# Nystrom attention and a multiplicative FFN: loads of q, k and v cut in pieces between other work, and the first batch's turns moved

## The chip, the cores and the metric

The kernel runs on one core of one Trainium2 chip. The core has five engines that run side by side and wait for one another by semaphores: TensorE (PE in the profile), VectorE (DVE), ScalarE (ACT), GpSimd (POOL) and SyncE (SP). The metric is the device time of one execution in microseconds (us).

## The reference

```python
B, H, S, D = 8, 8, 576, 64;  m = 32;  scale = 1 / 8
q_lm = q.reshape(B, H, m, S // m, D).mean(axis=3)     # 32 landmarks of 18 rows each
k_lm = k.reshape(B, H, m, S // m, D).mean(axis=3)
A, Bm, C = sm(q, k_lm), sm(q_lm, k_lm), sm(q_lm, k)   # softmax of the scaled products
Z = Bm.T / (norm1(Bm) * norminf(Bm) + 1e-6)
for _ in range(6): Z = 2 * Z - Z @ Bm @ Z
attn = A @ Z @ C @ v                                  # per batch and head
x = attn with the heads side by side                  # (4608, 512)
out = (((x @ w1) * (x @ w2)) @ w3) @ w_out            # w1, w2: 512x1024, w3: 1024x1024, w_out: 1024x512
```

All inputs and the output are float32 in memory.

## The kernel before

The work is written out by hand in one order; each engine takes its instructions in the order in which the program issues them, and a tile framework adds the waits. Work is staged by batch, eight batches of 8 heads x 576 rows.

- **Loads.** `load_qk` (L71) brings k and then q of a batch from GpSimd's DMA queue, changing them to float16 on the way, 96 partitions x 8 heads x 384 values. `load_v` (L77) brings v in float32 from SP's queue. Each has two buffers.
- **Turns.** q and k are needed with the head's dimension on the partitions. For batch 0 TensorE turns them (`turn_on_pe`, L100, copied out by L104); for the others SP issues DMA transposes (`transposes`, L89, called by `turn_all`).
- **Landmark sums.** `landmarks` (L166 to L175) adds up the rows of each landmark in six operations into `parts`, once for k and once for q: on GpSimd, or, for q of batch 0, on VectorE in two halves.
- **Attention.** `attention` is a generator of 18 steps; between its steps the caller puts other work on TensorE. Its first step (L183) multiplies `parts`, so it needs the sums of both q and k. Steps 3 and 4 hold the scores of C (L224) and GpSimd's `presum` of them (L235 to L240, then L259 and L262), steps 6 and 7 the product with v (L305), steps 8 to 13 the six iterations (L369), and the last four (L412 to L418) fold the result into w1 and w2 to give `g`.
- **Up.** `up(st, j, w)` (L426) multiplies `g` by the first factor for unit j of 8. The product for w1 is copied out by ScalarE (L430), and VectorE multiplies it by the product for w2 into `ab` (L432). The products use three PSUM buffers named `big`.
- **Down.** `down` (L446) multiplies `ab` by w3 @ w_out, scaled out by ScalarE (L452) and written by SP (L459). An even batch has 8 half products, an odd one 10.
- **Fold.** `fold` makes w3 @ w_out (`w34`) in the first stage, once: 64 steps (`product`, L490), with turns of w3 on TensorE (`turn`, L477, copied out by L482 and L483).

The first stage issues the loads of the weights, of q and k of batch 0, and then mixes the fold's steps with the turns, sums and attention of batch 0. Two one-column copies on GpSimd (L565, L571) read q or k of batch 0 and write into the buffer of a load that follows, so that this load waits for them: a gate. After it, the loop over batches runs `up(b)` with attention of batch b+1 between the units, then the sums for batch b+2, then `down(b)` with the rest of attention b+1, and at its end the first step of attention b+2 (`steps(nxt)`).

Of the kernel before, what the change touches and what calls it, by code (L numbers as in the profile page):

```python
# [7 lines left out]
FP32 = mybir.dt.float32  # L8
FP16 = mybir.dt.float16
# [4 lines left out]
B = 8  # L14
H = 8
# [6 lines left out]
DF = 1024  # L22
# [3 lines left out]
NP = 96  # L26
# [5 lines left out]
def kernel(  # L32
# [11 lines left out]
    nc = tc.nc  # L44
    consts = ctx.enter_context(tc.tile_pool(name="consts", bufs=1))
    wpool = ctx.enter_context(tc.tile_pool(name="wpool", bufs=1))
    pin = ctx.enter_context(tc.tile_pool(name="pin", bufs=2))
# [5 lines left out]
    def big():  # L53
        return psp.tile([128, 2, 512], FP32, name="big", bufs=3)
# [13 lines left out]
    def load_qk(st, b):  # L68
        qkn = pin.tile([128, 2, H, 384], FP16, name="qkn")
        for t, src in ((1, k), (0, q)):  # L70
            nc.gpsimd.dma_start(out=qkn[0:NP, t, :, :],  # L71
                                in_=src[b].rearrange("h (p r) d -> p h (r d)", p=NP))
        st["qkn"] = qkn

    def load_v(st, b):
        vt = st["vt"] if "vt" in st else pin.tile([128, H, 384], FP32, name="vt")
        nc.sync.dma_start(out=vt[0:NP], in_=v[b].rearrange("h (p r) d -> p h (r d)", p=NP))  # L77
        st["vt"] = vt

    def load_weight(t, w):  # L80
        for qd in range(2):
            nc.gpsimd.dma_start(out=wup[64 * qd:64 * qd + 64, :, t, :],
                                in_=w[256 * qd:256 * qd + 256, :].rearrange("(h d) j -> d h j", d=D))
# [10 lines left out]
    def turn_on_pe(st, t, h0, copy):  # L94
        if "qkT" not in st:
            st["qkT"] = pat.tile([128, 2, H, 3, NP], FP16, name="qkT")
        ps = psp.tile([128, 2, 1024], FP16, name="big", bufs=3)
        for i in range(2):
            for n in range(6):
                nc.tensor.transpose(  # L100
                    out=ps[:, i, NP * n:NP * n + NP],
                    in_=st["qkn"][0:NP, t, h0 + 2 * i + n // 3, 128 * (n % 3):128 * (n % 3) + 128],
                    identity=ident16[0:NP, 0:NP])
        copy(out=st["qkT"][:, t, h0:h0 + 4, :, :].rearrange("p (i h) c s -> p i (h c s)", i=2),  # L104
             in_=ps[:, :, 0:6 * NP])
# [49 lines left out]
        return mask4, par, ones, eye2, iit, onesq, selc, lomask  # L155


    def landmarks(st, t, eng=nc.gpsimd):
        if "parts" not in st:
            st["parts"] = pz.tile([128, 2, 2, H, 32], FP16, name="parts")  # L160
        for h0 in ((0,) if eng is nc.gpsimd else (0, 4)):
            own, n = ("", H) if eng is nc.gpsimd else ("v", 4)
            hs = slice(h0, h0 + n)
            x = st["qkT"][:, t, hs, :, :]
            tr = pat.tile([128, n, NP], FP32, name="tr" + own, bufs=1)
            eng.tensor_tensor(out=tr, in0=x[:, :, 0, :], in1=x[:, :, 1, :], op=ALU.add)  # L166
            eng.tensor_tensor(out=tr, in0=tr, in1=x[:, :, 2, :], op=ALU.add)  # L167
            t3 = tr.rearrange("p h (l g) -> p h l g", g=3)
            o = pat.tile([128, n, 32], FP32, name="o3" + own, bufs=1)
            hi, lo = st["parts"][:, 0, t, hs, :], st["parts"][:, 1, t, hs, :]  # L170
            eng.tensor_tensor(out=o, in0=t3[:, :, :, 0], in1=t3[:, :, :, 1], op=ALU.add)
            eng.tensor_tensor(out=o, in0=o, in1=t3[:, :, :, 2], op=ALU.add)  # L172

            eng.tensor_copy(out=hi, in_=o)
            eng.tensor_tensor(out=lo, in0=o, in1=hi, op=ALU.subtract)  # L175
# [334 lines left out]
    sts = [dict() for _ in range(B)]  # L510

    def turn_all(b):
        for t in (1, 0):
            for h0 in (0, 4):
                transposes(sts[b], t, range(h0, h0 + 4))

    def steps(g, n=1):
        for _ in range(n):
            next(g, None)
# [3 lines left out]
    with tc.tile_pool(name="pf", bufs=2) as pf:  # L523
        wof, w3f = {}, {}
        wsp = pf.tile([128, 2, 8, DM], FP16, name="wsp", bufs=1)

        def load_w3(j, cc=None):
            if j not in w3f:
                w3f[j] = pf.tile([128, DF], FP32, name="w3f", bufs=3)
            sl = slice(0, DF) if cc is None else slice(512 * cc, 512 * cc + 512)  # L530
            nc.sync.dma_start(out=w3f[j][:, sl], in_=moe_w3[128 * j:128 * (j + 1), sl])

        def load_wout(i, eng):
            wof[i] = pf.tile([128, 2, DM], FP32, name="wof", bufs=3)
            eng.dma_start(out=wof[i],
                          in_=moe_w_out[256 * i:256 * i + 256, :].rearrange("(c p) f -> p c f", p=128))

        load_w3(0, 0)
        load_wout(0, nc.scalar)
        load_w3(1, 0)  # L540
        load_wout(1, nc.scalar)
        load_w3(0, 1)
        load_wout(2, nc.scalar)
        load_w3(1, 1)

        warm = pf.tile([128, 512], FP16, name="warm", bufs=1)
        nc.vector.memset(warm, 0.0)
        psw = big()
        for _ in range(10):
            nc.tensor.matmul(psw[:, 0, :], warm[:, 0:128], warm, start=True, stop=True)  # L550

        nc.gpsimd.tensor_copy(out=gate, in_=wof[1][:, 0, 0:1])
        load_qk(sts[0], 0)
        load_weight(0, moe_w1)
        load_weight(1, moe_w2)
        mask4, par, ones, eye2, iit, onesq, selc, lomask = constants()
        fd = fold(pf, wof, w3f, wsp)
        steps(fd, 1)
        load_wout(3, nc.sync)
        load_w3(2)  # L560
        steps(fd, 6)
        load_w3(3)
        steps(fd, 9)
        w3f[4] = pf.tile([128, DF], FP32, name="w3f", bufs=3)
        nc.gpsimd.tensor_copy(out=w3f[4][0:NP, 0:1], in_=sts[0]["qkn"][0:NP, 1, 0, 0:1])  # L565
        load_w3(4)
        turn_on_pe(sts[0], 1, 0, nc.scalar.copy)
        turn_on_pe(sts[0], 1, 4, nc.vector.tensor_copy)
        landmarks(sts[0], 1)
        sts[0]["vt"] = pin.tile([128, H, 384], FP32, name="vt")  # L570
        nc.gpsimd.tensor_copy(out=sts[0]["vt"][0:NP, 0, 0:1], in_=sts[0]["qkn"][0:NP, 0, 0, 0:1])  # L571
        load_v(sts[0], 0)
        load_qk(sts[1], 1)
        steps(fd, 8)
        turn_on_pe(sts[0], 0, 0, nc.scalar.copy)
        turn_on_pe(sts[0], 0, 4, nc.vector.tensor_copy)
        landmarks(sts[0], 0, nc.vector)
        steps(fd, 3)
        load_w3(5)
        steps(fd, 4)  # L580
        at = attention(sts[0])
        for n, m in enumerate((2, 2, 2, 2, 2, 2, 2, 1, 1, 1, 1, 1, 1, 1, 2, 2, 2, 2, 2, 1)):
            steps(at)
            if n == 3:
                load_w3(6)
            elif n == 7:
                load_w3(7)
                load_v(sts[1], 1)
                turn_all(1)
                landmarks(sts[1], 1)  # L590
                load_qk(sts[2], 2)
                landmarks(sts[1], 0)
            steps(fd, m)
        steps(at, 30)
        steps(fd, 64)
    pab = ctx.enter_context(tc.tile_pool(name="pab", bufs=3))
    at = attention(sts[1], acc)


    for b in range(B):  # L600
        st = sts[b]
        ab = st["ab"] = pab.tile([128, 8, S], FP16, name="ab")
        if b + 2 < B:
            turn_all(b + 2)
            load_v(sts[b + 2], b + 2)
        if b % 2 == 0:
            chunks = [[(b, ab, 128 * t, 128)] for t in range(4)]
        else:
            chunks = [[(b - 1, sts[b - 1]["ab"], 512, 64), (b, ab, 0, 64)]]
            chunks += [[(b, ab, 64 + 128 * t, 128)] for t in range(4)]  # L610
        for j in range(8):
            up(st, j, 0)
            steps(at, (0, 0, 1, 1, 1, 1, 1, 2)[j] if b == 0 else 1)
            up(st, j, 1)
        if b + 3 < B:
            load_qk(sts[b + 3], b + 3)
        if b + 2 < B:
            landmarks(sts[b + 2], 1)
            landmarks(sts[b + 2], 0)
        nxt = attention(sts[b + 2], acc) if b + 2 < B else iter(())  # L620
        hold = {}
        nd = 2 * len(chunks)
        for n in range(nd):
            bank = (lambda: big()[:, 0, :]) if n // 2 % 2 else acc
            down(chunks[n // 2], n % 2, hold, bank)
            steps(at, 2 if n == 6 and nd == 8 or b == 0 and n > 3 else 1)
        steps(at, 30)
        steps(nxt)
        at = nxt
# [30 lines left out]
```

## Time and profile before

| | |
|---|---|
| Median of 3 runs | 295.22 us |
| The runs | 296.96, 295.16, 295.22 us |
| The profiled execution | 296.96 us; span from first to last instruction 294.9 us |
| Mean granted TensorE clock | 0.986 |
| PE, DVE, POOL, ACT busy | 277.5, 174.1, 141.7, 123.7 us |
| First stage, until the first up unit | 0 to 77.9 us |
| One even and one odd batch (batches 1 and 2) | 105.9 to 160.9 us |

A row of a timeline has the start in the span, the time it took, the engine, the line of the program, the operation, and the tiles it writes and reads with their shapes. In a list of waits, "A <- B" means that A stood idle until B was done. A row of a group ends in its count, its busy time in all, the mean of one in ns, and the idle time before. A row of a DMA issue ends in KB and in us from issue to landing.

### The profile page before, as it was taken

The page shows a single profiled execution, that of the slowest core. Times are in us where ns is not written, and L with a number is a line of the kernel's source. Part 1 is how long each engine was busy: PE and PEld are TensorE (multiplying, and loading weights), DVE is VectorE, ACT ScalarE, POOL GpSimd, SP SyncE. Part 2 cuts the span into 40 slices and gives each one's busy share as a digit, 9 for nine tenths or more (in the row PEclk, how much of TensorE's full clock was granted, in tenths as well). Part 3 has the DMA queues.
Part 4 walks back from the last instruction along what each step waited for, and adds up shares of the span by engine and source line. Part 5 has one row for each costly group of instructions (what it writes and reads, how often), then busy time and mean ns, then how long its engine had stood idle before and what let it go on. Part 6 is the DMA issues. An engine that isn't in the chain of part 4 may idle for free.

```text
span 294.9 us, 9448 instructions
## 1 busy us (share of the span) xinstructions
PE 277.5 (94%) x4026; PEld 152.7 (52%) x4026; DVE 174.1 (59%) x442; ACT 123.7 (42%) x199; POOL 141.7 (48%) x184
## 2 busy tenths in 40 slices
PE   8799789999999899999999999999999999999993
PEld 3355346544575357436743764376457435744641
DVE  7843733374474676656765765476666665665720
ACT  2114234215272366146525732573266236625531
POOL 1705405097049929942993599059909931500000
PEclk9799979999999999999999999999999999999999
DMA  7899999919956849947996999389949532012124
GB/s 238 279 235 242 219 259 259 182 35 178 175 133 87 186 104 186 210 132 111 175 227 165 146 224 189 100 167 203 221 116 169 119 107 71 4 37 74 37 65 113
DMA packets 61385, 45.56 MB, mean 154 GB/s; under 512 B 34976, under 2 KB 53408, under 8 KB 61344
## 3 DMA queue, kind: packets, MB, share of 16 engines
q1 hardware_dynamic: 46896, 31.86, 49.2%
q0 software_dynamic: 13632, 11.54, 25.0%
q10 hardware_dynamic: 816, 1.57, 1.5%
q8 instruction: 31, 0.51, 0.7%
q14 instruction: 10, 0.08, 0.1%
HBM read 38.80 MB, written 9.44 MB: 164 GB/s over the span
## 4 chain that ended last, share of the span: by engine, by line
PE 82%; DVE 9%; ACT 6%; issue 2%; DVEq 0%; ACTq 0%
PE big L426 17%; PE acc L446 13%; PE acc L490 12%; PE big L446 10%; PE big L412 6%; DVE ab L432 4%; PE big L369 4%; ACT a_sb L430 3%; PE small L305 2%; PE big L477 2%; PE small L490 2%; PE acc L305 2%; PE big L224 2%; PE big L550 2%; PE big L353 1%
## 5 line engine op out<-in xcount | busy, mean ns | idle before, releaser
L426 PE MATMUL big<-ahat,gt 128*128 128x288 f16 x512 | 74.1, 286 | 2.5 <-ACT a_sb L430 1.7
L432 DVE TENSOR_TENSOR ab<-a_sb,big 128x576 f16<-128x576 f16 x64 | 48.0, 750 | 19.6 <-PE big L426 8.4
L426 PEld LDWEIGHTS <-gt 128*128 128x128 f16 x512 | 47.1, 98 | 19.1 <-issue 4.1
L430 ACT CAST a_sb<-big 128x576 f16<-128x576 f32 x64 | 41.0, 640 | 36.7 <-PE big L426 35.9
L235 POOL TENSOR_TENSOR t<-ect 96x384 f32<-96x384 f32 x16 | 15.9, 994 | 79.3 <-ACT ect L228 78.6
L490 PE MATMUL acc<-wsp,w3t 128*128 128x512 f16 x168 | 43.4, 394 | 5.4 <-DVE w3t L483 2.7
L446 PE MATMUL acc<-w,ab 128*128 128x512 f16 (+1 forms) x192 | 41.0, 382 | 0.1
L446 PEld LDWEIGHTS <-ab 128*128 128x128 f16 (+1 forms) x320 | 24.0, 100 | 32.7 <-issue 9.8
L446 PE MATMUL big<-w,ab 128*128 128x512 f16 x128 | 32.8, 381 | 0.2 <-DVE ahat L356 0.2
L490 PEld LDWEIGHTS <-w3t 128*128 128x128 f16 x192 | 18.4, 101 | 25.9 <-issue 6.7
L166 POOL TENSOR_TENSOR tr<-qkT 128x768 f32<-128x768 f16 x15 | 24.6, 1642 | 11.5 <-DMA qkT<-qkn 6.6
L418 DVE TENSOR_SCALAR gt<-big 128x1024 f16<-128x1024 f32 x16 | 19.6, 1225 | 17.9 <-PE big L412 17.9
L452 ACT ACTIVATE o_sb<-acc 128x512 f32<-128x512 f32 x20 | 11.9, 597 | 38.5 <-PE acc L446 35.7
L167 POOL TENSOR_TENSOR tr<-tr,qkT 128x768 f32<-128x768 f32 x15 | 24.6, 1641 | 1.2
L483 DVE SCALAR_TENSOR_TENSOR w3t<-big,w3t 128x512 f16<-128x512 f32 x16 | 11.1, 691 | 18.9 <-ACT w3t L482 18.9
L482 ACT ACTIVATE w3t<-big 128x512 f16<-128x512 f32 x16 | 9.5, 596 | 25.6 <-PE big L477 20.7
L416 ACT ACTIVATE gt<-big 128x1024 f16<-128x1024 f32 x16 | 16.4, 1024 | 7.9 <-PE big L412 7.9
L412 PE MATMUL big<-wup,zt 64*32 64x512 f16 x512 | 19.3, 381 | 0.0
L452 ACT ACTIVATE o_sb<-big 128x512 f32<-128x512 f32 x16 | 9.6, 597 | 21.8 <-PE big L446 21.8
L228 ACT ACTIVATE ect<-big 96x768 f32<-96x768 f32 x16 | 12.9, 807 | 3.3 <-PE big L224 2.9
L356 DVE TENSOR_TENSOR ahat<-eat,big 128x576 f16<-128x576 f16 x16 | 11.9, 749 | 1.2 <-PE big L353 1.2
L172 POOL TENSOR_TENSOR o<-o,tr 128x256 f32<-128x256 f32 x15 | 12.0, 800 | 1.2
(313 smaller groups left out, 358.5 us busy)
## 6 DMA issues: line engine op xcount, KB each, us to landing
vt<-in_v_dram SPq DMA_DIRECT2D x8, 1152.0 KB, 8.7
qkn<-in_k_dram POOLq DMA_DIRECT2D x8, 576.0 KB, 10.5
qkn<-in_q_dram POOLq DMA_DIRECT2D x8, 576.0 KB, 13.2
out_dram<-o_sb SPq DMA_DIRECT2D x24, 192.0 KB, 2.3
w3f<-in_moe_w_dram SPq DMA_DIRECT2D x6, 512.0 KB, 8.0
out_dram<-o_sb SPq DMA_DIRECT2D x24, 128.0 KB, 2.3
wup<-in_moe_w_dram POOLq DMA_DIRECT2D x4, 512.0 KB, 18.4
wof<-in_moe_w_out_dram ACTq DMA_DIRECT2D x3, 512.0 KB, 7.5
```

What stands on the lines that cost most here:

```text
L166: eng.tensor_tensor(out=tr, in0=x[:, :, 0, :], in1=x[:, :, 1, :], op=ALU.add)
L167: eng.tensor_tensor(out=tr, in0=tr, in1=x[:, :, 2, :], op=ALU.add)
L235: nc.gpsimd.tensor_tensor(out=t3[0:NP], in0=e[:, :, 0:3, :], in1=e[:, :, 3:6, :], op=ALU.add)
L412: nc.tensor.matmul(psG[32 * h:32 * h + 32, qd, :], zt[rs, i, h, :], wup[rs, h, w, fs], start=(i == 0), stop=(i == 1), tile_position=(64 * ...
L416: nc.scalar.activation(out=g[:, :, w, fs], in_=psG, func=AXF.Copy, scale=1.0 / ZS)
L418: nc.vector.tensor_scalar(out=g[:, :, w, fs], in0=psG, scalar1=1.0 / ZS, scalar2=None, op0=ALU.mult)
L426: nc.tensor.matmul(p[:, c, 0:HS], st["g"][:, qd, w, 128 * j:128 * j + 128], st["ahat"][qd][:, c, :], start=(qd == 0), stop=(qd == 1))
L430: nc.scalar.copy(out=st["a_sb"], in_=p[:, :, 0:HS])
L432: nc.vector.tensor_tensor(out=st["ab"][:, j, :].rearrange("p (c s) -> p c s", c=2), in0=st["a_sb"], in1=p[:, :, 0:HS], op=ALU.mult)
L446: nc.tensor.matmul(pso[o:o + sz, :], ab[:, j, s0:s0 + sz], w34[:, j, :], start=(j == 0), stop=(j == 7), tile_position=(0, o))
L452: nc.scalar.activation(out=o_sb, in_=pso[:, :], func=AXF.Copy, scale=1.0 / (X64 * X64))
L490: nc.tensor.matmul(psW[j][:, :], turned[j, c // 4][:, a, c % 4, :], wsp[:, b, c, :], start=(c == 0 and a + b == 0), stop=(c == 7 and a == 1))
```

## The change

In the steady part, v of a batch is loaded in four pieces of two heads, each behind a gate that reads a column of `ab` of an up unit (units 3 to 6); before, it was one load behind the transposes. q and k of batch b+3 are loaded in eight pieces that GpSimd issues between the operations of the sums for batch b+2; before, there were two loads ahead of these sums.

In the first stage, v of batch 0 is loaded behind the third block of w3, with no gate; the gate on w3's block 4 goes too. k of batch 0 is turned after 13 fold steps (before: 16) and q after 17 (before: 24), and attention of batch 0 starts after 24 (before: 31) and has two fold steps in each gap. The sums for q of batch 1 go from GpSimd to VectorE, behind up unit 0 of batch 0, and attention of batch 1 is spread a little differently.

```diff
     def load_v(st, b):
-        vt = st["vt"] if "vt" in st else pin.tile([128, H, 384], FP32, name="vt")
+        vt = pin.tile([128, H, 384], FP32, name="vt")
         nc.sync.dma_start(out=vt[0:NP], in_=v[b].rearrange("h (p r) d -> p h (r d)", p=NP))
         st["vt"] = vt
+
+    def load_v_piece(st, b, i, done):
+        if i == 0:
+            st["vt"] = pin.tile([128, H, 384], FP32, name="vt")
+        hs = slice(2 * i, 2 * i + 2)
+        nc.gpsimd.tensor_copy(out=st["vt"][0:NP, 2 * i, 0:1], in_=done)
+        nc.sync.dma_start(out=st["vt"][0:NP, hs],
+                          in_=v[b, hs].rearrange("h (p r) d -> p h (r d)", p=NP))
+
+    def qk_pieces(st, b):
+        st["qkn"] = pin.tile([128, 2, H, 384], FP16, name="qkn")
+        for t, src in ((1, k), (0, q)):
+            for i in range(4):
+                hs = slice(2 * i, 2 * i + 2)
+                nc.gpsimd.dma_start(out=st["qkn"][0:NP, t, hs, :],
+                                    in_=src[b, hs].rearrange("h (p r) d -> p h (r d)", p=NP))
+                yield
...
-    def landmarks(st, t, eng=nc.gpsimd):
+    def landmarks(st, t, eng=nc.gpsimd, pieces=iter(())):
...
+            next(pieces, None)
             eng.tensor_tensor(out=tr, in0=x[:, :, 0, :], in1=x[:, :, 1, :], op=ALU.add)
+            next(pieces, None)
             eng.tensor_tensor(out=tr, in0=tr, in1=x[:, :, 2, :], op=ALU.add)
+            next(pieces, None)
             t3 = tr.rearrange("p h (l g) -> p h l g", g=3)
...
             eng.tensor_tensor(out=o, in0=t3[:, :, :, 0], in1=t3[:, :, :, 1], op=ALU.add)
             eng.tensor_tensor(out=o, in0=o, in1=t3[:, :, :, 2], op=ALU.add)
+            next(pieces, None)
 
             eng.tensor_copy(out=hi, in_=o)
             eng.tensor_tensor(out=lo, in0=o, in1=hi, op=ALU.subtract)
...
         load_w3(2)
-        steps(fd, 6)
+        load_v(sts[0], 0)
+        steps(fd, 11)
         load_w3(3)
-        steps(fd, 9)
-        w3f[4] = pf.tile([128, DF], FP32, name="w3f", bufs=3)
-        nc.gpsimd.tensor_copy(out=w3f[4][0:NP, 0:1], in_=sts[0]["qkn"][0:NP, 1, 0, 0:1])
-        load_w3(4)
+        steps(fd, 1)
         turn_on_pe(sts[0], 1, 0, nc.scalar.copy)
         turn_on_pe(sts[0], 1, 4, nc.vector.tensor_copy)
         landmarks(sts[0], 1)
-        sts[0]["vt"] = pin.tile([128, H, 384], FP32, name="vt")
-        nc.gpsimd.tensor_copy(out=sts[0]["vt"][0:NP, 0, 0:1], in_=sts[0]["qkn"][0:NP, 0, 0, 0:1])
-        load_v(sts[0], 0)
         load_qk(sts[1], 1)
-        steps(fd, 8)
+        steps(fd, 4)
+        load_w3(4)
         turn_on_pe(sts[0], 0, 0, nc.scalar.copy)
         turn_on_pe(sts[0], 0, 4, nc.vector.tensor_copy)
         landmarks(sts[0], 0, nc.vector)
-        steps(fd, 3)
-        load_w3(5)
-        steps(fd, 4)
+        steps(fd, 7)
         at = attention(sts[0])
-        for n, m in enumerate((2, 2, 2, 2, 2, 2, 2, 1, 1, 1, 1, 1, 1, 1, 2, 2, 2, 2, 2, 1)):
+        for n in range(20):
             steps(at)
-            if n == 3:
+            if n == 1:
+                load_w3(5)
+            elif n == 5:
                 load_w3(6)
-            elif n == 7:
+            elif n == 9:
                 load_w3(7)
                 load_v(sts[1], 1)
                 turn_all(1)
-                landmarks(sts[1], 1)
-                load_qk(sts[2], 2)
-                landmarks(sts[1], 0)
-            steps(fd, m)
-        steps(at, 30)
+            steps(fd, 2)
         steps(fd, 64)
+        landmarks(sts[1], 1)
+        load_qk(sts[2], 2)
...
         if b + 2 < B:
             turn_all(b + 2)
-            load_v(sts[b + 2], b + 2)
...
             up(st, j, 0)
-            steps(at, (0, 0, 1, 1, 1, 1, 1, 2)[j] if b == 0 else 1)
+            if b == 0 and j == 1:
+                landmarks(sts[1], 0, nc.vector)
+            steps(at, (0, 0, 0, 1, 1, 1, 2, 2)[j] if b == 0 else 1)
+            if b + 2 < B and j > 3:
+                load_v_piece(sts[b + 2], b + 2, j - 4, st["ab"][0:NP, j - 1, st.get("t0", 0):st.get("t0", 0) + 1])
             up(st, j, 1)
-        if b + 3 < B:
-            load_qk(sts[b + 3], b + 3)
         if b + 2 < B:
-            landmarks(sts[b + 2], 1)
-            landmarks(sts[b + 2], 0)
+            pieces = qk_pieces(sts[b + 3], b + 3) if b + 3 < B else iter(())
+            landmarks(sts[b + 2], 1, pieces=pieces)
+            landmarks(sts[b + 2], 0, pieces=pieces)
...
-            steps(at, 2 if n == 6 and nd == 8 or b == 0 and n > 3 else 1)
+            steps(at, 2 if n == 6 and nd == 8 else 1)
```

## The prediction

> **What bounds the kernel now.** I first read the busy shares, then who made TensorE (PE) wait, then the timeline of the engines around those places.
>
> ```profile
> PE 277.5 (94%) x4026; PEld 152.7 (52%) x4026; DVE 174.1 (59%) x442; ACT 123.7 (42%) x199; POOL 141.7 (48%) x184
> ```
>
> PE is busy nearly all the time, so whatever adds PE idle time adds to the end, and only PE's idle time can be won. The list of PE's waits (total, times, longest, us) shows how little there is:
>
> ```profile
> PE acc L490 <- DVE w3t L483: 2.7, 1, 2.7
> PE big L426 <- ACT a_sb L430: 1.7, 8, 0.2
> PE acc L199 <- ACT lm L188: 1.4, 6, 0.3
> ```
>
> Its one long wait is in the first stage. The windows around it (start:end and length, busy time of PE, PEld, DVE, ACT, POOL, then granted clock) show a second price:
>
> ```profile
> 34.60:37.40 2.80, 0.08 (x2) 0.02 (x1) 2.55 (x7) 0.00 (x0) 0.00 (x0) 1.00 1.08 228
> 37.40:40.00 2.60, 2.60 (x9) 1.62 (x10) 0.55 (x1) 0.60 (x1) 0.00 (x0) 0.52 1.16 248
> 40.00:42.00 2.00, 2.00 (x9) 0.82 (x8) 0.14 (x1) 0.35 (x1) 0.00 (x0) 0.78 1.10 291
> ```
>
> After 2.7 us of idle PE the clock is 0.52 and then 0.78 before it is full: 2.6 x 0.48 + 2.0 x 0.22 = 1.7 us more. The wait ends with VectorE's sums for q of batch 0:
>
> ```profile
> 31.89 0.55 DVE L166 TENSOR_TENSOR trv<-qkT 128x384 f32<-128x384 f16 x1
> 36.64 0.68 DVE L483 SCALAR_TENSOR_TENSOR w3t<-big,w3t 128x512 f16<-128x512 f32 x1
> ```
>
> From 31.89 to 36.64 VectorE does nothing but these sums (4.75 us), and the piece of w3 that PE needs stands behind them.
>
> **The steady part: where the change bites.** In the timeline of batch 2, GpSimd finishes its part of attention (L262), issues two loads, and makes the two sets of sums for batch 4:
>
> ```profile
> 142.96 0.72 POOL L262 TENSOR_TENSOR bmbd<-bmn,mask 128x256 f32<-128x256 f32 x1
> 143.62 0.81 POOL L71 DMA_DIRECT2D qkn<-in_k_dram  x1
> 144.43 0.77 POOL L71 DMA_DIRECT2D qkn<-in_q_dram  x1
> 145.21 1.65 POOL L166 TENSOR_TENSOR tr<-qkT 128x768 f32<-128x768 f16 x1
> ...
> 156.80 0.67 POOL L175 TENSOR_TENSOR parts<-o,parts 128x256 f16<-128x256 f32 x1
> ```
>
> The sums run 145.21 to 157.47, 12.26 us. Their reader is the first matmul of the next attention, which stands in PE's order behind batch 2's down products and ahead of batch 3's up units:
>
> ```profile
> 160.93 0.61 PE L183 MATMUL small<-parts,iit 128*128 128x512 f16 x2
> ```
>
> So there are 3.46 us to spare (160.93 - 157.47), and whatever makes the sums later than that stops PE.
>
> The change puts two things before their end. First, GpSimd's order now has four one-column copies, the gates, ahead of the loads and sums; the last reads the product (L432) of up unit 6, which is here:
>
> ```profile
> 147.36 0.76 DVE L432 TENSOR_TENSOR ab<-a_sb,big 128x576 f16<-128x576 f16 x1 [0.26 <-PE big L426]
> ```
>
> It ends at 148.12, not at 143.62 where GpSimd was free. Behind that gate wait the loads, the sums, and then PE. Second, eight loads are issued between the sums, in place of two ahead of them, and every one of them stands before the last two operations of its set. The two old issues cost 1.59 us together. The price t of a piece (96 partitions x 2 heads, 192 rows) isn't in the trace, so it is bounded by these groups:
>
> ```profile
> L71 POOL DMA_DIRECT2D qkn<-in_k_dram x8 | 6.7, 833 | 0.0
> L71 POOL DMA_DIRECT2D qkn<-in_q_dram x8 | 6.3, 783 | 0.0
> L82 POOL DMA_DIRECT2D wup<-in_moe_w_dram x4 | 2.5, 642 | 0.0
> ```
>
> L71 moves 768 rows in about 0.8 us, L82 256 rows (64 partitions x 4) in 0.64. If price goes with bytes, a piece costs a quarter of L71, 0.2 us. If it is all fixed, 0.8. A line through both sizes gives 0.64 - 64 x (0.16/512) = 0.62; I take 0.61, close to L82, whose row count is nearest.
>
> The trace shows 0.64 us for an issue a third as long as one of 0.8. The Trainium skill (DMA: Bandwidth & Descriptors, "Anatomy of one DMA — SWDGE (gpsimd) path") says that many descriptors can be emitted before their number starts to cost; the same page ("Rules for kernel authors") advises coalescing transfers, which speaks against cutting these. Taken strictly, a piece would cost as much as a whole load, and the sum below would be that of rival C.
>
> From up unit 6's end, the new chain is gate 0.3 (two copies of this size, L565 and L571, took 0.18; plus the handover) + sums 12.26 + 8 x 0.61 = 17.4 us. The room, from that product's end to the first matmul (L183), is in the timeline for the five batches that load ahead: batch 0 89.20 to 105.49, 16.3; batch 1 119.25 to 134.26, 15.0; batch 2 12.8; batch 3 174.68 to 190.33, 15.65; batch 4 204.18 to 217.03, 12.85. PE therefore stalls 1.2 + 2.4 + 4.6 + 1.8 + 4.6 = **14.6 us**. With t = 0.2 the chain is 14.2 and only batches 2 and 4 stall, 2.7 us. With 0.8 it is 19.0 and the sum 22.2. Batch 5 has gates and no loads: 12.6 against 14.9, nothing.
>
> Each stall past about 2.1 us also costs clock: idle bits of 1.26 and 0.88 us near 8 us were followed by 1.7 us of lost clock as well, while the 0.74 us wait at 98 lost none. After a stall the up phase comes, which by the chain is about 18% ScalarE and VectorE (6.8% of the span in L430 and L432, over eight phases of some 13.5 us, 37% of the span), so 1.7 x 0.82 = 1.4. Three stalls (batches 1, 2, 4): **4.2 us**, bounds 0 and 5 x 1.7 = 8.5.
>
> The trace shows the half clock after 2.7 us. The Trainium skill (TensorE: Matmul & The Clock Gate, "Part 1: The HAM clock gate") puts the idle window at about 3.4 us; by it batch 1 would lose nothing, and the sum would be 1.4 us smaller.
>
> **Batch 0: sums on VectorE.** The sums for q of batch 1 move from GpSimd (66.30 to 72.49 there, hidden) to VectorE, between the products of up units 0 and 1. They take 4.75 us by the rows at 31.89. Unit 0's product ends at 80.11; PE has only three PSUM buffers, so it can finish unit 2 and no more, at about 81.3; unit 1's product now ends at 80.11 + 4.75 + 0.76 = 85.6. PE idles 4.3 us where it had some 0.1, and the clock costs 1.4: **5.6 us** (4.2 + 1.4). Bounds: 1.0, if later waits of VectorE (3 us idle up to 91) take up most of it, and 6.5.
>
> **First stage.** v of batch 0 (1.15 MB) is now in SP's queue at about 10.6 us with no gate, ahead of w3's rows 3 and 4; k is turned after 13 fold steps, not 16, and q after 17, not 24. By the timeline step 13 ends at 20.5; k's turn (1.04), four steps and two turns of w3 bring q's to 25.0. Landings in a free queue and in a crowded one, from issue at 9.70 (k) and 10.65 (q):
>
> ```profile
> qkn<-in_k_dram POOLq DMA_DIRECT2D x1, 576.0 KB, 10.2
> qkn<-in_q_dram POOLq DMA_DIRECT2D x1, 576.0 KB, 12.2
> ```
>
> ```profile
> qkn<-in_k_dram POOLq DMA_DIRECT2D x1, 576.0 KB, 13.9
> qkn<-in_q_dram POOLq DMA_DIRECT2D x1, 576.0 KB, 19.0
> ```
>
> The first pair was beside three loads of w3 and w_out, the second (31.25 and 32.05) beside v. So k lands at 19.9 to 23.6 and q at 22.9 to 29.7; k waits 0 to 3.1 us, q then 0 to 1.6. I take 1.5 for both, nearer the first pair, because SP's queue is full in both until 19.5. Then PE has seven steps and a turn, 5.0 us, over a VectorE chain of 5.5 (31.2 to 36.7): 0.6 us of wait. So -2.7 - 1.7 + 0.6 + 1.5 = **-2.3 us**, bounds -3.8 (both on time) and +2.6 (both late, and the clock with them). The attention of batch 0 starts 7 steps earlier with two fold steps in each gap; its waits were 0.2 us, so nothing. v's pieces later have a whole batch to land, 27 us against 8.7: nothing either; if late, the matmul of L305 would wait. On SP, v's four issues now wait for the gates, and behind them stand the output writes of the same batch; the first of these has data only some 3 us after the last gate (93.69 against 89.20 in batch 0), so that wait is covered, and without that cover the output buffers (three) would fill and ScalarE would wait.
>
> **The sum.** -2.3 + 5.6 + 14.6 + 4.2 = +22.1. The profiled execution took 296.96 (span 294.9 and 2.1 around it), which gives 319.1; the other two runs took 295.16 and 295.22, so on the median it is 317.3. I forecast 317.
>
> **Rivals.**
> A: a piece's issue goes with its bytes (0.2 us). For it: L82 is cheaper than L71. Against: by far not in proportion. -2.3 + 5.6 + 2.7 = +6.0, 301.
> B: the pieces cost GpSimd nothing, because the issue runs beside the sum before it; this decides below t = 0.03, where the chain fits batch 2's 12.8 us. For it: GpSimd's spans are rough. Against: 143.62, 144.43, 145.21, start to start, with nothing overlapping. The stalls vanish: +3.3, and with the first stage at its good end +1.8, 297, no change; it is faster only if VectorE's sums also fall to their lower bound.
> C: a piece costs a whole issue, 0.8. All five stalls pass 2.1 us: -2.3 + 5.6 + 22.2 + 5 x 1.4 = +32.5, 328.
> D: v ahead delays k and q to the crowded landings. +2.6 in place of -2.3: 322. For it: DMA share above 1 from 15 us on.
> That the gates hold nothing is ruled out by GpSimd's order alone: the copy reads what up unit 6 writes.
>
> **How the numbers follow.** Forecast 0.58 (own range 311 to 323, from t of 0.5 to 0.7 and the clock's bounds), A 0.17, B 0.08, C 0.10, D 0.07. From 300 to 327 leaves out B and most of C, under 2 in 10. A measurement here tells about 1% (3 us) from no change: faster 0.02 and same 0.07 are B and A's low edge; slower 0.91.
>
> **What would show it.** In the changed profile: PE waiting at the first matmul of attention for GpSimd's sums (parts), 4 to 5 us in batches 2 and 4 and half that in batch 1; granted clock near 0.5 after them; a piece's issue at 0.6 us; PE idle about 4 us for VectorE's product early in batch 0; the 2.7 us wait of the first stage gone. If the sums end before PE comes to them, the forecast is wrong.

## The result, and the profile after

The changed kernel takes 319.61 us (median of four runs, 318.58 to 320.10); the kernel before, on the same chip, 295.62 us (295.16 to 296.96). The ratio is 1.0799, 95% interval 1.0752 to 1.0846: 24 us slower. The forecast was 317. The profiled execution took 318.58 us, with a span of 316.8 and a mean clock of 0.959 (0.986 before).

The busy shares of after come first (busy us, share of the span, instructions):

```profile
PE 283.5 (89%) x4026; PEld 155.0 (49%) x4026; DVE 178.5 (56%) x454; ACT 124.9 (39%) x199; POOL 156.4 (49%) x230
```

TensorE has as many instructions as before and 6 us more of busy time, as a lower clock would make; its share fell from 94% to 89%. GpSimd has 46 instructions more and 14.7 us more of work. Who makes TensorE wait (us in total, times, longest):

```profile
PE small L204 <- POOL parts L195: 13.0, 5, 3.6
PE small L204 <- DVE parts L195: 2.7, 2, 2.4
PE big L117 <- DMA qkn<-in_k_dram: 2.1, 1, 2.1
...
PE small L204 <- POOL parts L196: 1.4, 5, 0.4
...
PE big L117 <- DMA qkn<-in_q_dram: 0.7, 1, 0.7
```

The five waits at L204 (the first matmul of attention, L183 before) for GpSimd's sums are new, one in each of batches 0 to 4, and so are those at L117 for k and q of batch 0. The row for VectorE's `parts` holds two waits: 2.4 us in the up phase of batch 0, for the sums for q of batch 1, and 0.3 us in the first stage. The 2.7 us wait for a turn of w3 is gone.

This is GpSimd's timeline in batch 2 of after, the place that the prediction showed of before:

```profile
157.13 0.18 POOL L84 CAST vt<-ab 96x1 f32<-96x1 f16 x1 [1.39 <-DVE ab L453]
157.37 0.69 POOL L93 DMA_DIRECT2D qkn<-in_k_dram  x1
158.07 1.65 POOL L184 TENSOR_TENSOR tr<-qkT 128x768 f32<-128x768 f16 x1
...
172.45 0.66 POOL L93 DMA_DIRECT2D qkn<-in_q_dram  x1
173.11 0.41 POOL L195 CAST parts<-o 128x256 f16<-128x256 f32 x1
173.61 0.66 POOL L196 TENSOR_TENSOR parts<-o,parts 128x256 f16<-128x256 f32 x1
```

Before the first row GpSimd stood idle until VectorE's product of up unit 6 (L453) was done: the last gate. Then an issue stands ahead of nearly every operation of the sums, which end at 174.27, 17.1 us after the gate began. In TensorE's timeline the reader waits for them:

```profile
173.58 0.38 PE L204 MATMUL small<-parts,iit 128*128 128x512 f16 x1 [3.62 <-POOL parts L195]
174.33 0.38 PE L204 MATMUL small<-parts,iit 128*128 128x512 f16 x1 [0.37 <-POOL parts L196]
```

The two waits, 3.99 us, are the stall of batch 2: TensorE starts on the first half of `parts` (L195) and then waits for the second (L196). The windows around it (start:end and length; busy us of PE, PEld, DVE, ACT, POOL; granted clock, DMA share, GB/s):

```profile
169.90:173.60 3.70, 0.08 (x9) 0.10 (x2) 1.23 (x1) 0.16 (x1) 3.53 (x6) 1.00 0.93 155
173.60:175.00 1.40, 1.03 (x5) 0.46 (x5) 0.00 (x0) 0.26 (x1) 0.66 (x1) 0.85 1.27 211
175.00:177.00 2.00, 2.00 (x17) 1.06 (x16) 1.08 (x3) 1.09 (x3) 0.00 (x0) 0.50 1.85 136
177.00:179.00 2.00, 1.92 (x20) 1.53 (x19) 1.11 (x3) 1.04 (x2) 0.00 (x0) 0.75 1.03 229
```

Little but GpSimd works during the stall, and afterwards the clock is 0.85, 0.50 and 0.75.

Measured from first up unit to first up unit, the stages of the two profiled executions are (us):

| | first stage | batch 0 | 1 | 2 | 3 | 4 | 5 | rest |
|---|---|---|---|---|---|---|---|---|
| before | 77.94 | 27.99 | 28.76 | 26.68 | 29.39 | 26.71 | 28.65 | 48.78 |
| after | 75.00 | 36.02 | 31.48 | 32.04 | 32.32 | 30.95 | 30.34 | 48.65 |
| difference | -2.94 | +8.03 | +2.72 | +5.36 | +2.93 | +4.24 | +1.69 | -0.13 |
| by the prediction's steps | -2.3 | 6.8 | 2.4 | 6.0 | 3.2 | 4.6 | 1.4 | 0 |

The stall at the end of a batch costs its clock in the next, so the clock of batch 4's stall shows in batch 5.

### The profile page after: what moved, and what is told of

Read it like the earlier page. It is cut to its first block, busy times and chain, and to the rows that moved or that the text cites. A ratio compares the mean times of both kernels' runs of the same rounds, so it can differ in the third digit from the quotient of the medians.

```text
span 316.8 us, 9556 instructions
## 1 busy us (share of the span) xinstructions
PE 283.5 (89%) x4026; PEld 155.0 (49%) x4026; DVE 178.5 (56%) x454; ACT 124.9 (39%) x199; POOL 156.4 (49%) x230
## 4 chain that ended last, share of the span: by engine, by line
PE 47%; POOL 27%; DMA 8%; DVE 8%; issue 5%; ACT 4%; ACTq 0%; DVEq 0%; POOLq 0%
PE big L447 15%; PE acc L511 9%; POOL qkn L93 8%; DMA qkn<-in_q_dram 5%; POOL tr L186 5%; POOL tr L184 5%; PE acc L467 5%; DVE ab L453 4%; PE big L467 4%; POOL o L192 2%; DMA wof<-in_moe_w_out_dram 2%; PE big L433 2%; POOL o L191 2%; PE small L326 2%; ACT a_sb L451 2%
## 5 line engine op out<-in xcount | busy, mean ns | idle before, releaser
L447 PE MATMUL big<-ahat,gt 128*128 128x288 f16 x512 | 80.9, 304 | 2.9 <-ACT a_sb L451 1.3
L447 PEld LDWEIGHTS <-gt 128*128 128x128 f16 x512 | 49.7, 103 | 25.2 <-issue 8.5
L453 DVE TENSOR_TENSOR ab<-a_sb,big 128x576 f16<-128x576 f16 x64 | 47.9, 750 | 23.2 <-PE big L447 12.2
L511 PE MATMUL acc<-wsp,w3t 128*128 128x512 f16 x168 | 42.1, 384 | 1.2 <-DVE wsp L492 0.9
L184 POOL TENSOR_TENSOR tr<-qkT 128x768 f32<-128x768 f16 x14 | 23.0, 1646 | 20.2 <-DMA qkT<-qkn 11.0
L84 POOL CAST vt<-ab 96x1 f32<-96x1 f16 x24 | 4.3, 182 | 42.1 <-issue 21.8
L186 POOL TENSOR_TENSOR tr<-tr,qkT 128x768 f32<-128x768 f32 x14 | 23.1, 1651 | 0.5
L204 PE MATMUL small<-parts,iit 128*128 128x512 f16 x16 | 6.6, 432 | 17.1 <-POOL parts L195 13.0
L211 DVE TENSOR_TENSOR qbd<-lm,par 128x512 f16<-128x512 f16 x8 | 5.5, 692 | 19.4 <-ACT lm L209 19.4
```

What stands on the lines that cost most here:

```text
L447: nc.tensor.matmul(p[:, c, 0:HS], st["g"][:, qd, w, 128 * j:128 * j + 128], st["ahat"][qd][:, c, :], start=(qd == 0), stop=(qd == 1))
L453: nc.vector.tensor_tensor(out=st["ab"][:, j, :].rearrange("p (c s) -> p c s", c=2), in0=st["a_sb"], in1=p[:, :, 0:HS], op=ALU.mult)
L511: nc.tensor.matmul(psW[j][:, :], turned[j, c // 4][:, a, c % 4, :], wsp[:, b, c, :], start=(c == 0 and a + b == 0), stop=(c == 7 and a == 1))
```

## Experiments

**My theory**: the gates start GpSimd's chain of sums late, the eight issues between the sums stretch it, and TensorE stops at L204 for what exceeds its room; VectorE's sums in batch 0 cost some 5 us more. **Rivals**: the pieces' traffic or late landing is what hurts, not their issue; the gates alone, or the pieces alone, do it all; the clock after stalls costs nothing.

### Gates and pieces, apart and together

**e1**: after, with q and k loaded whole ahead of the sums; the gates stay.

```diff
-            pieces = qk_pieces(sts[b + 3], b + 3) if b + 3 < B else iter(())
-            landmarks(sts[b + 2], 1, pieces=pieces)
-            landmarks(sts[b + 2], 0, pieces=pieces)
+            landmarks(sts[b + 2], 1)
+            landmarks(sts[b + 2], 0)
# and, ahead of both:
+        if b + 3 < B:
+            load_qk(sts[b + 3], b + 3)
```

> Changed kernel (319.6 us) with the gates kept, but k and q of batch b+3 loaded whole, two issues ahead of the sums. Theory (GpSimd's chain of gate, issues and sums holds PE): the chain falls from 17.9 us (0.24 + 8 x 0.67 + 12.3) to 14.1 (0.24 + 1.6 + 12.3), so of 14.4 us of stalls at the first matmul of attention some 3 stay (batches 2 and 4 at 1.3, batch 0 at 0.4), and about 4 us of lost clock go with the others: 304 us. Rival (the gates alone, or the traffic of loads that arrive while v and the transposes do, hold it): no more than 3 us gained, 316 us or more.

Measured 302.81 us, ratio 1.0222 (1.017 to 1.0274). The stalls that are left at L204 for GpSimd are 0.22 us in batch 0, 1.26 in batch 2 and 1.25 in batch 4.

**e2**: after, with v loaded whole behind `turn_all` and no gates; the pieces of q and k stay.

```diff
         if b + 2 < B:
             turn_all(b + 2)
+            load_v(sts[b + 2], b + 2)
...
-            if b + 2 < B and j > 3:
-                load_v_piece(sts[b + 2], b + 2, j - 4, ...)
```

> Changed kernel with the eight pieces of k and q kept between the sums, but v loaded whole behind the transposes and no gates, so that the chain starts when GpSimd has finished its part of attention. Theory: batch 2's chain starts at 152.55 in place of 157.37 and ends near 170.2, PE comes at 169.95: 0.3 us of stall there and in batch 4, none in 1 and 3; batch 0 keeps its 2.9 us, because there the gates end before GpSimd is free anyway. 319.6 - 11 - 4 of clock = 305 us. Rival (eight small transfers as such are the cost, by issue or by late landing): the stalls stay, 316 us or more.

Measured 308.42 us, 1.0409 (1.0355 to 1.0463): slower than I expected. The stalls at L204 behave as they should (only batch 0 keeps one, 2.50 and 0.37 us), but TensorE has a new one in batch 1. Its timeline:

```profile
127.09 0.40 PE L390 MATMUL big<-sz__1715,tz__1716 32*32 32x96 f32 x16 [3.81 <-issue]
```

"issue" means that nothing the profile shows held it. The clock then is 0.60 and 0.53 until 131. The DMA queues of e2 from 112 to 124 (packets, MB, share of 16 engines):

```profile
q1 hardware_dynamic: 5199, 2.19, 102.3%
```

and from 124 to 127.1, of the same view:

```profile
q1 hardware_dynamic: 88, 0.11, 17.7%
q8 instruction: 1, 0.02, 2.8%
```

While v's one load of 1.15 MB and the transposes fill the engines there is no packet of the instruction queue; one comes when they are through, and TensorE goes on. That suggests that TensorE waited for instructions. It needed a run of its own.

**e10**: after, with v's four gates on units 0 to 3 in place of 3 to 6; the pieces of q and k stay.

```diff
-            if b + 2 < B and j > 3:
-                load_v_piece(sts[b + 2], b + 2, j - 4, st["ab"][0:NP, j - 1, ...])
+            if b + 2 < B and 0 < j < 5:
+                load_v_piece(sts[b + 2], b + 2, j - 1, st["ab"][0:NP, j - 1, ...])
```

> Changed kernel with the four gates reading up units 0 to 3 in place of 3 to 6, pieces kept. The last of them is open at about 1 us before GpSimd is free, so they delay nothing, as in the kernel without gates (308.4 us); but v comes in four parts and not at once. Theory (in that kernel, 3.8 us in batch 1 in which PE waited for nothing the profile shows, and the half clock after it, came from PE's instructions being fetched behind v's one large load): that wait is absent, 303.5 us. Rival (the wait belongs to the place of the instructions, not to v's load): 308 us.

Measured 303.87 us, 1.0247 (1.0194 to 1.0301). There is no "issue" wait in batch 1 (29.52 us long, 33.66 in e2), and batches 2 and 4 are as short as before, 26.68 and 26.71; only batch 0 keeps its stall behind GpSimd, 2.8 us. So the wait of e2 is gone when v comes in pieces. The large load alone doesn't make it, though: the kernel before, e3 and e8 load v whole as well, and their longest "issue" waits are 0.4, 0.75 and 1.23 us, while e5 (next), with v in pieces, has one of 1.53. What else it takes is open. And the same four gates and the same eight issues that make after slow cost little if the gates open before GpSimd has finished its part of attention: it is the place of the gates that counts.

**e5**: after, with the gates kept and all eight pieces issued behind the last sum.

```diff
-            landmarks(sts[b + 2], 1, pieces=pieces)
-            landmarks(sts[b + 2], 0, pieces=pieces)
+            landmarks(sts[b + 2], 1)
+            landmarks(sts[b + 2], 0)
+            for _ in qk_pieces(sts[b + 3], b + 3):      # if b + 3 < B
+                pass
```

> Changed kernel with the same gates and the same eight pieces, but all pieces issued behind the two sets of sums. Theory (the issues stand in GpSimd's order ahead of what PE waits for): the chain is 0.24 + 12.3 = 12.5 us, batch 2's sums end at 169.7 where PE comes at 169.95: no stalls behind GpSimd's sums, their 14.4 us and 4 to 5 us of clock come back: 301 us. Rival (the number of transfers, or when they land, matters): traffic and sizes are unchanged and the loads land later, so 315 us or more.

Measured 303.65 us, 1.0227 (1.018 to 1.0273). No stall behind GpSimd is left, though the same pieces now take longer to land (medians 5.5 and 6.4 us; 4.0 and 4.3 in after). Traffic and late landing therefore aren't the cause: their rival falls. The 2.6 us above my expectation hold a 1.5 us "issue" wait and one of 1.5 us at L390 for ScalarE.

**e3**: after, with neither gates nor pieces (the edits of e1 and e2 together).

> Changed kernel with neither gates nor pieces: loads as in the kernel before, but the first stage and VectorE's sums for batch 1 as changed. Theory: all stalls behind GpSimd's sums go (14.4 us) and their clock (4 to 6): 300 us, of which VectorE's sums hold about 5 and the first stage gives back 2 to 3 against 295.6. Rival: if the first stage or VectorE's sums were a larger part than that, 305 or more is left.

Measured 301.66 us, 1.0185 (1.014 to 1.0231). Batch 0 takes 32.34 us against 27.99 before, and batches 2 and 4 are as before.

By ratios, over e3: the gates alone +0.4% (e1), the pieces alone +0.6% (e10, gates out of the way), both +6.0% (after). The first two carry some 0.7% of uncertainty each, so they can't be told from nothing. The room swallows nearly all of either, not of both.

### The price of an issue

**e6**: after, with each piece cut in two: 16 issues of 96 rows in a batch, the same bytes. (Two issues now stand at each of the eight places.)

```diff
-                hs = slice(2 * i, 2 * i + 2)
-                nc.gpsimd.dma_start(...)
+                for u in range(2):
+                    hs = slice(2 * i + u, 2 * i + u + 1)
+                    nc.gpsimd.dma_start(...)
                 yield
```

> Changed kernel with every piece cut in two: two issues of one head each where one issue of two heads stood. Theory (an issue costs GpSimd a nearly fixed time; 0.79 us for 768 rows and 0.665 for 192 give 0.62 + 0.00022 x rows, so 0.64 for 96): 16 x 0.64 = 10.3 us in place of 5.3, 5 us more in each of five batches and the clock in batch 3 too: 346 us. Rival (issue goes with bytes or rows): 320 us.

Measured 337.73 us, 1.139 (1.1311 to 1.1468). The direction is the theory's; the size is 8 us short, and the group of k's issues in e6 (count, busy us, mean ns, idle before) says why:

```profile
L94 POOL DMA_DIRECT2D qkn<-in_k_dram x40 | 20.7, 522 | 0.2
```

beside that of after:

```profile
L93 POOL DMA_DIRECT2D qkn<-in_k_dram x20 | 13.4, 668 | 0.2
```

q's issues are the same within 2%. Sixteen take 8.2 us in a batch and eight 5.3; I had expected a second full price for each cut. The 2.9 us more, times five, are 14.6 of the 18.1 us between the two medians, and the stalls at the first matmul of attention come to 28.3 us in all, 13.9 more than in after. The first stage, which the edit doesn't touch, took 3.2 us longer in e6's profile than in after's (78.18 and 75.00 us). With the 0.8 us of a whole load, an issue has a large fixed part and a small one by rows: 0.52 us at 96 rows, 0.66 at 192, 0.80 at 768, which isn't one straight line either.

### The clock

**e7**: after, with 10, 5, 14, 5 and 13 matmuls whose result nobody reads, put ahead of `steps(nxt)` in batches 0 to 4, so that TensorE is busy in the stalls.

> Changed kernel with idle matmuls of 128x512 put into PE's order ahead of the first matmul of attention, 10, 5, 14, 5 and 13 of them for batches 0 to 4, into a PSUM buffer that nothing reads. They fit in the stalls (0.216 us each). Theory (the stall costs clock besides): granted clock stays at 1.0 behind the stalls, and 1.2 to 1.4 us for each of batches 0, 1, 2 and 4 come back: 314.5 us. Rival (the up phase waits for ScalarE and VectorE, so half clock costs nothing there): 319.6 us.

Measured 316.33 us, 1.0685 (1.0629 to 1.0742). The window of e7 behind batch 2's stall:

```profile
175.00:177.00 2.00, 1.82 (x28) 1.51 (x29) 1.83 (x6) 1.27 (x4) 0.00 (x0) 1.00 1.30 239
```

The clock is 1.00 where after had 0.50, and batches 1 to 5 take 30.80, 30.82, 31.16, 30.82 and 28.65 us (31.48, 32.04, 32.32, 30.95 and 30.34 in after). The half clock is worth 319.61 - 316.33 = 3.3 us; the two ratios' intervals lie just apart (1.0742 and 1.0752). It is a cost of its own, and the rival that it is none falls. Its size is less sure: batches 1 to 5 of the two profiles differ by 4.9 us, but e7's first stage took 2.0 us longer than after's.

### Batch 0 and the first stage

**e4**: after, with the sums for q of batch 1 back on GpSimd.

```diff
-            if b == 0 and j == 1:
-                landmarks(sts[1], 0, nc.vector)
# first stage:
         landmarks(sts[1], 1)
         load_qk(sts[2], 2)
+        landmarks(sts[1], 0)
```

> Changed kernel with only the sums for q of batch 1 back on GpSimd. Theory: batch 0's up phase was 18.4 us against 13.4 before, so 5 us come back, and 1 us more because batch 0's sums for batch 2 then start earlier against PE: 313.5 us. Rival (PE would have waited there anyway, for GpSimd or the transposes, so VectorE's sums cost little): 318 us.

Measured 313.22 us, 1.0574 (1.0526 to 1.0621): 6.4 us less than after. In the profile, batch 0 is 5.0 us shorter (30.99 us). Batch 0's stall stays (2.73 and 0.16 us), so the 1 us that I expected from it isn't there; batch 2 is 1.1 us shorter instead, because the clock stayed at 1.00 behind batch 1's stall.

**e8**: before, with the first stage of after alone: the edits of e3 and e4 together (and after's spreading of attention in batch 0), that is no gates, no pieces and the sums on GpSimd.

> Kernel before with only the changed first stage (v of batch 0 early and without a gate, turns after 13 and 17 steps, attention after 24) and the changed steps in batch 0, the sums for batch 1 on GpSimd: neither gates nor pieces nor VectorE's sums. Theory: the 2.7 us wait and its clock go, waits for k and q of 2 to 4 us and their clock come: 1 to 3 us faster than before, 294 us. Rival (v ahead of k and q costs as much as it brings): 296 us, no change.

Measured 296.35 us (ten runs) against 295.75, 1.0024 (0.9981 to 1.0066): no change, as the rival had it, where I expected a gain. TensorE waits 1.6 us for k and 1.7 for q, more than the wait for w3's turn that went away. Between e8 and e3 stand only VectorE's sums: 1.6%, 4.8 us.

**e9**: before, with the turn of k after 15 fold steps and of q after 17, attention after 24 with two fold steps in each gap; v stays gated on q.

```diff
-        steps(fd, 9)           # ahead of the turn of k
+        steps(fd, 8)
...
-        steps(fd, 8)           # ahead of the turn of q
+        steps(fd, 2)
...
-        for n, m in enumerate((2, 2, 2, 2, 2, 2, 2, 1, 1, 1, 1, 1, 1, 1, 2, 2, 2, 2, 2, 1)):
+        for n, m in enumerate((2,) * 20):
```

> Kernel before with its loads and gates unchanged (v of batch 0 behind q), but k turned after 15 fold steps (16 before), q after 17 (24), attention of batch 0 from step 24 (31) with two fold steps in each gap. Theory (the first stage's gain is the turn's place, and v's early load is what the changed kernel pays for it): k (19.9) and q (22.85) are there when PE comes, the 2.7 us wait and its 1.7 us of clock go, 0.6 us comes: 3 to 3.5 us faster than before, 292.3 us. Rival (q's turn at step 17 waits for its load with or without v, or the clock at the start decides): 295 us.

Measured 295.39 us (twelve runs) against 296.76, 0.9958 (0.9925 to 0.999): faster by 0.4%, less than I expected. k and q come in time, but TensorE's longest wait is now

```profile
PE small L183 <- DVE parts L174: 2.3, 1, 2.3
```

and VectorE's timeline shows the sums for q taking longer in their first half than in their second, of the same shapes:

```profile
26.22 1.25 DVE L166 TENSOR_TENSOR trv<-qkT 128x384 f32<-128x384 f16 x1
...
28.41 0.83 DVE L171 TENSOR_TENSOR o3v<-trv 128x128 f32<-128x128 f32 x1
...
30.59 0.55 DVE L166 TENSOR_TENSOR trv<-qkT 128x384 f32<-128x384 f16 x1
```

Until 30.26 GpSimd makes the sums for k beside them, and two of its operations are slower too: L171 takes 0.83 us there and 0.63 elsewhere, L172 1.01 and 0.79. Moving q's turn up to k's put the two engines' sums side by side; the second half, alone, takes the 0.55 us of the kernel before.

### A faster version

**e11**: e9, and v in four pieces with gates on units 0 to 3 as in e10; q and k whole, the sums on GpSimd.

> The kernel with the early turns and, besides, v of batches 2 to 7 in four pieces behind gates on up units 0 to 3; q and k whole, ahead of the sums, as before. Theory: gates at units 0 to 3 don't delay GpSimd, and the 0.7 us that batch 3 loses to an unexplained PE wait in the kernel before goes: 291.6 us, 0 to 1 us faster than without the pieces. Rival (gates among the presums delay the sums, or v lands too late): slower than without the pieces.

Measured 293.12 us (six runs, 291.55 to 293.93) against 296.76, 0.9877 (0.9832 to 0.9921). It beats both kernels.

**e12**: before, with v in four pieces gated on units 0 to 3, and nothing else.

> Kernel before with one part of the change in a form that delays nothing: v of batches 2 to 7 in four pieces behind gates on up units 0 to 3, all else as before. Theory (the pieces only take v's burst off PE's instruction fetch, which cost the kernel before 0.7 us in batch 3): 295 to 296 us, 0 to 1 us faster. Rival (v in pieces is worth the whole 2.3 us that lay between the two kernels with early turns): 293.5 to 294.5 us.

Measured 295.22 us (twelve runs) against 296.33, 0.9947 (0.9917 to 0.9978). Batch 3 takes 28.65 us in place of 29.39, the others as before. The two halves, 0.9958 and 0.9947, multiply to 0.9905, inside e11's interval, so the gain of e11 need be no more than both; but their intervals are too wide to share out its 3.6 us.

## Why the prediction was right, point by point

By ratios to before, at 295.6 us, the parts add up as follows: first stage +0.7 us (e8), VectorE's sums +4.8 (e3 over e8), gates +1.1 (e1 over e3), pieces behind the gates +17.1 (after over e1). The first has 1.3 us of uncertainty and the others about 2, so the first stage's part and the gates' can't be told from nothing. Set against the prediction's sum, the stalls and their clock are right (18.8 predicted, 18.2 measured), VectorE's sums nearly so, and the first stage is 3 us off; the forecast of 317 missed by 2.6.

- **Stalls behind GpSimd: 14.6 predicted, 14.4 measured** (13.0 + 1.4, the lines above). The mechanism is shown from three sides: with the gates out of the way (e10) 2.8 us of stalls are left, with the issues behind the sums (e5) none, with whole loads in place of the pieces (e1) 2.7; with twice the issues they grow to 28.3 (e6). Three terms of the chain were off and cancel in part. The issue took 0.66 us, not 0.61. The sums took 11.5 us between the issues, not 12.26. And TensorE starts when the first half of `parts` is there, so the chain counts to L195's end, 0.75 us earlier, before it waits 0.37 for the rest. So batches 1 to 4 together stalled 11.5 us where 13.4 was predicted. That the total still comes out is luck: batch 0's stall was longer by nearly as much.
- **Batch 0's share of them was mis-sized**: 1.2 predicted, 2.95 measured (2.79 + 0.16). The step that failed is the room counted from up unit 6's product. That product ends at 91.23 in after, but GpSimd was still at attention's own work:

```profile
92.71 0.72 POOL L283 TENSOR_TENSOR bmbd<-bmn,mask 128x256 f32<-128x256 f32 x1
93.38 0.30 POOL L84 CAST vt<-ab 96x1 f32<-96x1 f16 x2
93.68 0.69 POOL L93 DMA_DIRECT2D qkn<-in_k_dram  x1
```

  In this timeline of GpSimd the gates run back to back with no idle time, 2.15 us after the product: here they cost nothing but their 0.3 us. The kernel before shows most of it already:

```profile
89.69 0.73 POOL L262 TENSOR_TENSOR bmbd<-bmn,mask 128x256 f32<-128x256 f32 x1
```

  There GpSimd is free at 90.4, 1.2 us behind the product's end at 89.20, from which the prediction counted the room. The change's spreading of attention in batch 0 added the other 1.0: in e8, which has the spreading without gates and VectorE's sums, GpSimd is free 2.2 us behind the product.
- **Clock after stalls: 4.2 predicted; by e7 3.3 from the medians and 4.9 from batches 1 to 5 of the profiles.** I had counted on three stalls (batches 1, 2 and 4); the clock fell behind four, those of batches 0, 1, 2 and 4. The prediction rightly went by its own row, 0.52 after 2.7 us, against the longer idle window of the Trainium skill (TensorE: Matmul & The Clock Gate, "Part 1: The HAM clock gate"): behind batch 1's stall, 1.46 and 0.37 us long, the clock was 0.72 and then 0.50 from 143 to 147. But my threshold of 2.1 us isn't borne out either, nor is any other: behind batch 3's stall, 1.49 and 0.37 us long, the clock was 1.00 throughout, and so it was in e4 behind batch 1's of 1.46 and 0.37 us.
- **VectorE's sums in batch 0: 5.6 predicted.** Batch 0's up phase grew from 13.39 to 18.37 us, 5.0; by e8 and e3 they cost 4.8 us and by e4, in after, 6.4 (1.1 of it in the clock of batch 2). The size is inside the bounds, but TensorE's wait isn't the one that was forecast, 4.3 us for unit 1's product:

```profile
81.65 0.72 PE L204 MATMUL small<-parts,iit 128*128 128x512 f16 x2 [2.40 <-DVE parts L195]
82.64 2.08 PE L447 MATMUL big<-ahat,gt 128*128 128x288 f16 x8 [0.27 <-DVE ab L453]
```

  TensorE got as far as half of unit 3, and then waited 2.40 us for the sums themselves, which the first matmul of attention of batch 1 reads, and only 0.27 us for unit 1's product. Behind these waits the clock was 0.50 from 83 to 85. The prediction looked only at VectorE's place in the up units and left out that attention reads the sums too.
- **First stage: -2.3 predicted, nothing gained in the timed runs** (+0.7 by e8, no change within its interval). The profiles give -2.94, but in the kernel before's window from 9 to 20

```profile
9.00:20.00 11.00, 10.23 (x44) 5.19 (x44) 8.41 (x10) 1.19 (x2) 4.99 (x7) 0.84 1.00 247
```

  the clock was 0.84 and in after's 1.00. The profiles of e4, e5, e6 and e8 have after's first stage and the same 0.84; there it takes 76.16, 77.21, 78.18 and 76.84 us, from 1.8 us less to 0.2 us more than the 77.94 of before. So some 1 to 3 us of the -2.94 are chance, and that it lies near -2.3 is luck. The failed term is the waits for k and q: 1.5 assumed, 2.09 + 0.68 = 2.8 in after, and 3.1 to 5.2 in the other runs with the same first stage. They come late because v is ahead of them, as rival D said: in e9, where v stays behind q, TensorE waits for neither. D's bound of 4.7 for both is passed in e2 and e10.
- **The rivals**: A (0.2 us an issue) and B (none) fall by the rows of L93. C (0.8) was nearer to the price than A, but 0.66 isn't a whole load's 0.8 and its 328 wasn't reached. The rule on coalescing that the prediction weighed (DMA: Bandwidth & Descriptors, "Rules for kernel authors") bears out in direction: eight issues of 0.66 us replaced two of 0.8.
- **Nothing predicted, nothing found**: v's pieces land in time, SP's writes cause TensorE no wait, batch 5 has no stall of its own (its +1.69 is the clock of batch 4's).

## What to carry to other kernels

A DMA issue took time of the engine that issued it, GpSimd here: 0.52 us for 96 rows and 0.80 for eight times as many. Count each one that stands ahead of a result somebody waits for, together with every gate, against the room that result has. Two small delays on one in-order engine can each nearly fit alone (0.4% and 0.6% here) and cost far more together (6.0%), so try them apart and together before judging either. Put gates where they open before the engine comes to them, and issues behind the last operation that another engine needs, and look on every engine, not only the one that bounds, for what a step that moves will run beside.

## What the runs showed of the hardware that I had not expected

- **TensorE can stand still while the profile shows nothing that it waits for.** In e2 it did for 3.81 us while v's load and the transposes had 102% of the DMA engines, and the instruction queue's packet came only when they were through. The wait went with v in gated pieces (e10). That the packet was TensorE's own code is argued from this order, not shown, and a whole load of v isn't enough: e3 and e8 have one too and lose 0.75 and 1.23 us at most.
- **VectorE and GpSimd were slower when both added**: in e9 0.55 became 1.25 us and 0.33 became 0.83 on VectorE, 0.63 became 0.83 on GpSimd.
- **The same idle time can cost clock or not**: 0.72 and 0.50 behind 1.46 + 0.37 us in batch 1 of after, 1.00 behind 1.49 + 0.37 us in its batch 3.
- **The clock of the first 20 us differs between executions**: 0.84 from 9 to 20 us in the profile of before and 0.85 in that of e9, 1.00 in those of after and e11. One profile of each isn't enough to price a change of that stage; the timed runs are.
